# A token-mixing kernel: the second token matrix and three of eight pairs of the first in fp32 matmuls, without splits into fp16 parts

## The chip, the cores and the metric

The kernel runs on one core of a Trainium2 chip. The metric is the device time of one execution in microseconds; the median of three runs is compared. Engines are named as the profile does: PE is TensorE (PEld its weight loads), DVE is VectorE, ACT is ScalarE, SP is SyncE, which here only issues DMAs.

## What is computed

The inputs are a sequence `u` of 2048 tokens by 512 channels, the parameters of a state-space layer, and four weight matrices. The output is `x + s * g`:

```python
x = A_u
xn = _layernorm(x, axis=-1)
s = _A_ref(xn, ...)          # per channel: y = causal convolution of xn with K, plus xn * Dskip
g = _silu(_B_ref(xn, B_w1, B_w2, B_w3, B_w4))
return x + s * g

# _B_ref(x, w1, w2, w3, w4):
h = _gelu(_layernorm(x, axis=-1) @ w1)
# g0..g3: the four quarters of h's channels, shifted by +1, -1, +2, -2 tokens
hs = jnp.concatenate([g0, g1, g2, g3], axis=-1) @ w2
x1 = x + hs
h2 = _gelu(_layernorm(x1, axis=-1) @ w3) @ w4
return x1 + h2
```

`w1` and `w2` (512 x 512 each) are called the first and the second token matrix here. `K[d, l]` is the real part of a sum over 128 states of `C * exp(dt * A * l) * dt * B`, and the convolution in the reference goes by an FFT over 4096 points.

## The kernel before, in words

All 2048 tokens stay in SBUF as `X`, 128 partitions by 16 slots `s` by 512 channels; token = 16 * partition row + slot in each half, so a shift by one or two tokens is a step to another slot, and only the six combinations that run over the end (`WRAPS`, `wrapped`, line 1095) need rows moved, into `hw`.

The token mixing (`token_mixing`, line 1200) goes over eight pairs of slots. `ln_first` normalises (statistics on DVE; `E.affine` on ACT or DVE). `x_pair(j)` brings the normalised pair into `xT`, channels on the partitions: for `j < HF` in fp32, by four PE transposes a slot and a copy out of PSUM; for the others it is first split into two fp16 parts (`x2h`: a scaled rounding, then a `scalar_tensor_tensor` on DVE for the rest) and transposed by a DMA. `h_pair(j)` multiplies by w1: for `j < HF` 16 fp32 matmuls of 256 columns, else 48 fp16 matmuls (three products of parts, `PASSES`) with `w1h`, the split weights from `first_weights`. Then comes Gelu into `h32`, and `hT`, the result split into two fp16 parts again (one `affine`, one `scalar_tensor_tensor`). `HF` is 1, so only the first pair is in fp32. `u_stage1` multiplies two slots by a 64-point transform in fp32 and stores the result to DRAM (`ue`, then `scr_Ud`, 32 stores).

`second_weights` (line 976) finds w2's scale and splits w2 into `w2h`. `hs_pair` (line 1108) then takes the shifted slots of `hT` as the weights of PE and streams `w2h`: for each of 16 slots 4 channel blocks times 3 products of 512 columns, 192 fp16 matmuls in all, into two banks of `pa` or `pb`; DVE adds them into `X` with the scale `a2`. `hs` in this document is this step.

Beside it run two other streams. `tables` makes the convolution kernel in 16 chunks of 32 channels: on DVE and ACT the waves (`wv`), on PE 64 small fp32 matmuls (`pc<-wv`) and, after a copy into `kev`, eight more (`kev,kk`). `weight_squares` and `prep` load w3 and w4 (`wst`), find their scale and split them (`w3h`, `w4h`). After the token mixing, `mlp` runs eight times: six steps of matmuls on `w3h`, Gelu (`g`), a split (`ghl`) and matmuls on `w4h`. `products` multiplies spectra (`uin`, `kin`, `pr`, `z1e`), `inverse` and `finish` end with the gate, the residual and the store.

The order of all this is not the order of the code. Each call is recorded as an operation by `Plan.add`, and `Plan.order` (line 300) issues them in the order of the long list of numbers `ORDER` (line 110): a number is an operation, and a letter behind it chooses ACT (`a`) or DVE (`v`) where both can do it. Each engine works through its own instructions in that order. All instructions are issued from one line, 315, so the profile's rows are told apart by the names of the tiles.

Of the kernel before, what the change touches and what calls it, by code (L numbers as in the profile page):

```python
# [19 lines left out]
P = 128  # L20
# [31 lines left out]
HF = 1  # L52
# [58 lines left out]
5 0 8 7 3 88 89 6 79 80 81 82 90 91 92 93 83 2 94 95 22 21 105 84 85 9 106 86 103 96a 87a 97a 31 78 104 107 108 109  # L111
110 98 122 10 123 111 112 113 114v 115v 100v 119v 99a 124 116a 120 11 125 19 126 4 127 16 20 36 117 128 129 130 131
132 133 135 101 102a 134 138a 140a 136 38 18 37 137 17 152 158a 154a 39 42 40 14 153a 72 73a 139 15 70 71a 41 44 43 45
147 148 142 596 46 143 141 597 24 23 170 172 176 157a 174 177 173 604 205 47 149 175 171 155 48 49 178 50 144 160 51
150a 145a 159 179 52 180 211a 210a 53 181 182 118 121 195 196 54 146 156 207a 206a 183 59 151 25 26 245 200 201 202 27
184 185a 186a 243 189a 28 55 208 239 60 241 164 197 190 198v 230 192a 242 213 188a 56 246 187a 193 212 236a 209 240
310 235a 232a 231a 274 191 308 244 214a 194 225 311 237 312 309 220 221 314 13 598 313 234 315 61 57 226 247 62 316
248 317 249 233 203a 63 250 318 319 58 251 76 215 65 217a 606 238 280a 279a 64 252 320 204 253 218 66 68 29 255v 321
254v 275a 67 276a 299 216 199 222 219 264 261a 599 322 227 324a 281 256v 282 305a 304a 69 74 631 325a 396 265 269 277
270 258v 223v 259 228v 262 257v 278 300a 224 266 167 161 75a 162 229 271 301v 77a 601 30 397 602 260 600 283v 263 286a  # L120
272v 343 267a 294 284 273 302 287 323a 303 344a 268 603 306 32 295 307 296 289 297v 345a 632 290 349a 609 285 605 348a
368 327a 328 288 330v 346 338 298 291 607 331 350 351 608 329 373a 292v 615 347 370a 610 369a 339 352v 332 374v 326v
355a 618 375 293 333 334 335 387 376 392a 398 399 168 611 633 336a 400 337 163 401 402 340 356 372 403 341v 404 612
353 613 405 371 354 614 389a 424 393a 342 388a 358 406 165 407 409 166 408 169 425 363 364 410 411v 413v 412 634 414
616 359 483 482 637 426 427 487 499 428 429 635 430 395 636 617 484 498 619 620 640 621 33 432 431 434 433 435 622 485
638 659 448 449 34 488 450 360 361a 357 639 436 377 378 500 35 438 437 451 642 452 453 503 653 454 365 366a 382 654
379 641 662 383 439 440 442 441 384 491 495 380a 444 385a 490 386 513 391 623a 624 367 381 486 446 445 655 455 492 443
447 460 517 456 461 421 422 362 457 462 501 423 418 419 458 463 496 656 657 658 512 476 459 493 420 464 465 12 514 518
625 626a 643 627a 628a 644 489 645a 525 394 466 494 506 504 515 467 505 660 629a 468 675 516 469 676 502 507a 519 677
477a 473 497 390 520 479 478 509 521 415 416 524 538 417 1 529 678 646 526 630 679 680 508 522 661 681 470 535 480a  # L130
523 588a 589a 539 592a 682 546 593a 481 540 647 648a 649a 650a 543 561 663 664 684 665 536a 474 651a 705 697 590 532
666 683 698 667a 668 533a 560 510a 547 591 594 707 708 595 669 710 565 798 799 819a 686 709 652 699 537 568 562 805
670a 471 701 800 671a 672a 673a 806 807 700 702 511 685 687 703 472 688 801a 534 704 812 813 551 548 711 554 802 803
712 555a 556 814 732 557 820a 821 822 827 828 569a 570 834 835 577 804 558a 559 713 574 808a 809 810 714 811 706 719
716 733 715 717 689a 690 815a 816 734 823a 575a 578a 576 475 829 830a 718 824a 691 674 692a 571 825 817 693a 572a 694a
695a 720 721 741 841 842 818 735 836 837a 831 738 737 736 722 723 826 848 849 754 855 724a 755 856 579 696 756 739 757
573 758 838 832 833 839 843a 725 740 759 850 726 727a 844 840 845 742 743 760 744 745 851a 852 857 858a 934 859 869a
# [49 lines left out]
class Plan:  # L187
# [229 lines left out]
def kernel(  # L417
# [897 lines left out]
```

## Time and profile before

| | |
|---|---|
| runs | 535.85, 534.35, 536.67 us; median 535.85 |
| the profiled execution | 536.33 us, its span 534.5 us |
| mean granted clock of PE | 0.965 |
| ACT_TABLE_LOAD on ACT | 54 |
| DMA issues w2 and w1 (`w`) | 4 of 512 KB |

A row of the profile that groups instructions reads: line, engine, operation, tile written <- tiles read, shape, count, then after the bar the group's busy time in us and the mean duration of one record in ns, then the idle time ahead of them and who ended it. Matmul records overlap, so the group's busy time over its count is the price of one, not the mean record. An fp32 matmul leaves two records. A row of the timeline begins with its start and its length in us. A row of the stages gives a stretch, its length and each engine's busy time in it.

### The profile page before, as it was taken

Reading aid. Unit: us, or ns where it says so; the run is one execution under the profiler, and the core shown is the slowest. Engines: PE = TensorE matmul, PEld = TensorE weight load, DVE = VectorE, ACT = ScalarE, POOL = GpSimd, SP = SyncE. Lnnn points to the kernel's source line nnn. Section 1 sums busy time; section 2 is a strip of 40 time slices with the busy share of each in tenths; the row PEclk is TensorE's granted clock in tenths of the full one; section 3 lists DMA queues with packets and bytes.
Section 4 is the critical chain, followed back from the end, with each engine's and each line's share of the span. In section 5 each row is a group of like instructions: output and inputs, shape, how many; then the busy total and the mean of one; then the engine's idle time right before and its main releaser. Section 6 shows DMA issues by size and latency. Waiting matters only on the chain.

```text
span 534.5 us, 14802 instructions
## 1 busy us (share of the span) xinstructions
PE 486.1 (91%) x6292; PEld 311.9 (58%) x6292; DVE 476.8 (89%) x773; ACT 417.1 (78%) x699; POOL 0.7 (0%) x6
## 2 busy tenths in 40 slices
PE   8876986879989989999999999999999999899984
PEld 8552754554536745756657665666656665566542
DVE  4999699999999999999999999999998588667466
ACT  4899789988799999999999999998874634352520
POOL 0000000000000000000000000000000000000000
PEclk9795989999889989999999999999999999999998
DMA  8797785875457454440354660877679999996997
GB/s 234 177 229 198 203 207 140 229 200 163 119 118 155 101 108 104 61 60 14 49 101 80 139 171 21 187 143 172 144 156 190 268 319 236 264 309 204 341 307 195
DMA packets 160658, 91.13 MB, mean 170 GB/s; under 512 B 102544, under 2 KB 151952, under 8 KB 160208
## 3 DMA queue, kind: packets, MB, share of 16 engines
q1 hardware_dynamic: 156064, 85.73, 64.4%
q10 hardware_dynamic: 4528, 4.46, 3.2%
q8 instruction: 49, 0.80, 0.7%
q14 instruction: 17, 0.14, 0.1%
HBM read 52.95 MB, written 29.36 MB: 154 GB/s over the span
## 4 chain that ended last, share of the span: by engine, by line
PE 42%; DVE 27%; ACT 18%; DMA 8%; issue 5%; SPq 0%; ACTq 0%; DVEq 0%
PE pb L315 14%; PE pa L315 14%; DVE wv L315 11%; PE pc L315 8%; ACT wv L315 7%; PE pd L315 5%; DVE X L315 4%; DMA x1T<-x1h 2%; ACT L315 2%; DVE ghl L315 2%; ACT ue L315 1%; DVE pr L315 1%; DMA zin<-scr_Zda 1%; DMA scr_Ud<-ue 1%; ACT wst L315 1%
## 5 line engine op out<-in xcount | busy, mean ns | idle before, releaser
L315 PE MATMUL pb<-x1T,w3h 128*128 128x256 f16 (+1 forms) x1056 | 125.3, 274 | 3.4 <-issue 1.3
L315 PE MATMUL pa<-w4h,ghl 128*128 128x512 f16 (+1 forms) x528 | 123.3, 382 | 0.0
L315 PEld LDWEIGHTS <-w3h 128*128 128x128 f16 (+1 forms) x1056 | 101.9, 100 | 30.0 <-issue 15.4
L315 PEld LDWEIGHTS <-ghl 128*128 128x128 f16 (+1 forms) x528 | 49.6, 98 | 61.1 <-issue 9.3
L315 ACT ACT_TABLE_LOAD x54 | 69.3, 1283 | 11.5 <-PE pb L315 4.3
L315 ACT ACTIVATE wv<-wv 128x2080 f32<-128x2080 int32 x32 | 63.0, 1968 | 1.7 <-DVE wv L315 1.6
L315 ACT ACTIVATE g<-pb,wsc 128x512 f32<-128x512 f32 (+1 forms) x48 | 31.0, 655 | 14.9 <-PE pb L315 9.3
L315 PE MATMUL pb<-xT,w1h 128*128 128x256 f16 x336 | 39.6, 279 | 0.0
L315 PEld LDWEIGHTS <-w1h 128*128 128x128 f16 x336 | 32.9, 100 | 9.4 <-issue 2.9
L315 DVE TENSOR_TENSOR wv<-wv,eg 128x2048 f32<-128x2048 f32 x16 | 36.5, 2281 | 0.5 <-ACT wv L315 0.5
L315 PE MATMUL pc<-wv 128*32 128x64 f32 x2048 | 34.3, 225 | 2.9 <-ACT k1e L315 1.4
L315 PEld LDWEIGHTS pc<-wv 128*32 128x32 f32 x2048 | 31.4, 113 | 8.7 <-issue 2.5
L315 DVE TENSOR_TENSOR wv<-mag,wv 128x2048 f32<-128x2048 f32 x16 | 36.5, 2280 | 0.0
L315 DVE SCALAR_TENSOR_TENSOR ghl<-g,wsc,ghl 128x512 f16<-128x512 f32 (+1 forms) x48 | 33.6, 700 | 0.6 <-ACT ghl L315 0.3
L315 ACT ACTIVATE wv<-wv,halfpi 128x2080 f32<-128x2080 f32 x16 | 32.8, 2050 | 0.1
L315 ACT ACTIVATE mag<-par 128x128 f32<-128x128 f32 x132 | 32.5, 461 | 0.0
L315 PEld LDWEIGHTS <-hT 128*128 128x128 f16 x174 | 17.2, 99 | 24.9 <-issue 6.1
L315 DVE TENSOR_TENSOR pr<-pd,kh 128x512 f32<-128x512 f32 x32 | 20.6, 683 | 7.5 <-PE pd L315 5.9
L315 ACT ACTIVATE ghl<-g,wsc 128x512 f16<-128x512 f32 (+1 forms) x37 | 25.4, 691 | 1.5 <-PE pa L315 1.4
L315 DVE BATCH_NORM_STATS2 stats<-X 128x6 f32<-128x512 f32 x32 | 21.3, 679 | 5.2 <-DMA X<-in_A_u_dram 5.2
L315 DVE TENSOR_TENSOR wv<-par,ev 128x1056 int32<-128x1056 f32 x16 | 20.0, 1248 | 5.7 <-PE pc L315 5.7
L315 PE MATMUL pb<-w2h,hT 128*128 128x512 f16 x87 | 21.1, 395 | 2.6 <-DVE X L315 2.6
(158 smaller groups left out, 845.7 us busy)
## 6 DMA issues: line engine op xcount, KB each, us to landing
wst<-in_B_w_dram SPq DMA_DIRECT2D x20, 512.0 KB, 4.2
scr_Ud<-ue SPq DMA_DIRECT2D x32, 256.0 KB, 3.1
uin<-scr_Ud SPq DMA_DIRECT2D x16, 512.0 KB, 5.2
scr_Kfa<-k1e SPq DMA_DIRECT2D x8, 512.0 KB, 5.6
cst<-c_gp SPq DMA_DIRECT2D x16, 256.0 KB, 4.3
kin<-scr_Kfa SPq DMA_DIRECT2D x8, 512.0 KB, 5.2
scr_Kfb<-k1e SPq DMA_DIRECT2D x8, 512.0 KB, 6.7
scr_Zda<-z1e SPq DMA_DIRECT2D x8, 512.0 KB, 4.5
```

Source lines behind the costliest of these rows:

```text
L315: ins = [getattr(self.engines[op.eng], name)(*args, **kw).ins for name, args, kw in op.calls]
```

## The change

`HF` goes from 1 to 3: pairs 1 and 2 of the first token matrix take the way of pair 0, fp32 with PE transposes. `h_pair` writes `hT` in fp32 straight from Gelu, without `h32` and without parts, for all eight pairs. The second token matrix is used in fp32 as it was loaded: `second_weights`, `w2h` and the scales `s2`, `i2`, `a2`, `sh` are gone, `hs_pair` issues 64 fp32 matmuls, and DVE adds without a scale. w2 is loaded to the place that `w2h` had. `hw` holds one fp32 part instead of two fp16 ones. `ORDER` is a new list.

```diff
-HF = 1
+HF = 3
...
 ORDER = """
-5 0 8 7 3 88 89 6 79 80 81 82 90 91 92 93 83 2 94 95 22 21 105 84 85 9 106 86 103 96a 87a 97a 31 78 104 107 108 109
+8 31 0 7 88 3 4 78 89 90 91 22 21 103 105 106 104 92 107 108 2 109 6 93 94 95 5 79 110 111 96a 100a 80 81 82 83 14 112
...
-    hw = at(gtile.o, [P, 6, 2, P], F16, "hw")
+    hw = at(gtile.o, [P, 6, P], F32, "hw")
...
-        load_w(w2, w2s, Slots(sblocks + 10 * K4, sblocks + 11 * K4), Q)
+        load_w(w2, w2s, w2place, Q)
...
-        V.tensor_scalar(sh, s1, 2.0 ** -10, None, op0=ALU.mult)
...
-    def second_weights():
-        due("wq2")
-        for k in range(2):
-            w = wides[2 + k]
-            A.activation(at(phB + 4 * K4, [P, 2, D], F32, "sq"), w, AF.Square, accum_out=ssq[:, 14 + k : 15 + k])
-        pow2_scale(ssq[:, 14:16], s2, i2, 2.0 ** 14)
-        V.tensor_scalar(a2, i2, i1, 2.0 ** 10, op0=ALU.mult, op1=ALU.mult)
-        for k in range(2):
-            w = w2place([P, 2, 2, D], F16, "w2h")
-            E.affine(w[:, :, 0], wides[2 + k], s2)
-            V.scalar_tensor_tensor(w[:, :, 1], wides[2 + k], s2, w[:, :, 0], op0=ALU.mult, op1=ALU.subtract)
-            w2h.append(w)
...
-        h = stile([P, 4, 2, 2, P], F16, "hT")
+        h = stile([P, 4, 2, P], F32, "hT")
...
-            h32 = wtile([P, 2, 2 * P], F32, "h32")
-            A.activation(h32, ph, AF.Gelu_apprx_tanh, scale=1.0 if j < HF else a1)
-            E.affine(hv[0], h32, sh)
-            V.scalar_tensor_tensor(hv[1], h32, sh, hv[0], op0=ALU.mult, op1=ALU.subtract)
+            hv = h[:, 2 * m2 : 2 * m2 + 2].rearrange("p m a t -> p m (a t)")
+            A.activation(hv, ph, AF.Gelu_apprx_tanh, scale=1.0 if j < HF else a1)
...
-                    for n, (lh, lw) in enumerate(PASSES):
-                        T.matmul(
-                            acc[i], w[:, lh], w2h[m // 2][:, m % 2, lw],
-                            start=m == 0 and n == 0, stop=m == 3 and n == 2,
-                        )
+                    T.matmul(acc[i], w, w2s[m], start=m == 0, stop=m == 3)
...
-            V.scalar_tensor_tensor(X[:, s], acc[i], a2, X[:, s], op0=ALU.mult, op1=ALU.add)
+            V.tensor_add(X[:, s], X[:, s], acc[i])
...
-        second_weights()
```

Where the new list moves instructions, the prediction shows the rows on SP and on PE. The SP rows shown there are those around the load of w_103, one half of w2, among the stores `scr_Ud` of stage 1; the PE rows are those around the small matmuls `pc<-wv` of the fourth chunk of tables, which stood behind the first matmuls on `w3h` and now stand ahead of them.

Before, on PE, where the second token matrix begins, each matmul has a row of its weights ahead of it:

```order
L315 MATMUL pb_94<-xT,w1h 128x256
L315 LDWEIGHTS hT
L315 MATMUL pa_92<-w2h,hT 128x512
L315 LDWEIGHTS hT
L315 MATMUL pa_92<-w2h,hT 128x512
```

And now, where the fp32 matmuls stand as one row each and the two halves of w2 follow each other:

```order
L312 MATMUL pb_93<-xT,w1h 128x256
L312 MATMUL pa_92<-w_103,hT 128x512 x2
L312 MATMUL pa_92<-w_104,hT 128x512 x2
L312 MATMUL pa_91<-w_103,hT 128x512 x2
L312 MATMUL pa_91<-w_104,hT 128x512 x2
L312 MATMUL pc_96<-wv 32x64 x64
```

Three rows of four blocks of fp16 parts have become one row for two blocks; the first chunk's table matmuls follow after the first pair of slots.

More of the change, by code (lines that the diff above doesn't have):

```diff
@@ L116 @@
[L116 to L125, printed above, removed]
@@ new lines @@
+113v 84 85 86 17 115v 44 16 42 114a 87a 15 41 43 97a 20 101 98 36 45 46 18 37 118a 72 102a 47 99v 116 48 50 9 51 121
+10 122 49 52 23 143 117a 123 53 124 125 54 119 24 164 170 166 171 140 168 25 73a 141 167 165 126 169 551 127 55 172
+128 59 173 120a 60 56 11 146 174 175 142 129 19 38 151a 176 27 61 177 57 130 178 39 179v 152a 180v 26 182v 183v 33
+148a 144 40 181v 184 186a 131 62 229 28 187 145 147a 192 161 204v 185a 231 154 158 290 188a 132 134 288 70 205 553 150
+149 230 292 156 227 153 195 197a 196v 200a 286 375 232 225 287 291 289 71a 293 228 226 294 543 233 295 162 234 544 296
@@ new lines @@
+133 235 201a 207a 189 208 373 297 298 199 136v 545 34 299 236 237 190 216 198 63 191 137 217a 193 210 374 202 300 138v
+218a 211 304v 203 221v 65 194 64 546 238 371 13 222a 66 68 206 256 135 220 239 219 376 212 139 554 213 67 242v 223
+240v 224 257a 258a 262a 261a 209 69 74 555 243v 30 75a 214 215 241v 259 260 277 244v 302v 250 251 278a 58 76 279a 253
+252 247v 263 157 264 283a 254 268v 282a 379 245 246 317 248 249 372 163 271 548 549 159 160 265a 547 280 269 550 77a
+380 272 556 557 301v 255 558 559 281 285 552 381 266 318a 319a 565 284 578 322a 323v 562 308v 274 275 270 329v 267 309
@@ new lines @@
+273 276 338 560 320 321 340a 561 579 314 325 324 377 339v 342 311 341 312 344a 303v 343a 353 580 330 581 29 346 563
+584 564 378 315 355a 354a 305a 306 382 566 395 567 430 434 587 583 582 345 585 429 568 383 384 358a 385 386 387 155
+431 326a 586 388 569 600 396 397 601 570a 359a 446 389 390 606 445 316 391 392 602 35 393 394 407 589 310 398 408 409
+447 410 313 450 307 603 605 435 332 604 399 400 327 411 412 333 335 451 413 32 571 588 12 572 573a 336 401 334 432 609
+402 590 591 592a 607 331 448 337 328 622 360 623 361 453 608 347 403 624 348 611 350 351 349 362 438 404 414 610 631
@@ new lines @@
+711 712 846 809 731 700 824 825 826 732 810 811 853 847 800 801 812a 713 714 715a 880 854 807 808 813 814 831 815 832
+855 716 821a 856 857 849 923 717 718a 838 719a 499 848 819 850 851 822 827a 833 852 823 733 734 858 859 735 736 737a
+828 829 830 496 1215 839 860 861 834a 488 720a 721a 477 862 901 902 1222 1223 863 1216 1217 491 840a 474 835 903 738
+739 722 740a 741a 836 837 864 867 1224 865 1229 742a 743a 744 1218a 841 866 1236a 842 1225a 882 904 1230 1231 843 1244
+868 869 870 1219 871 906 844 1220 1221 907 872a 944 945 905 873 874 910 875a 876a 1251 946 1226 877a 878a 883 881
@@ new lines @@
+1237a 1232a 1227 885a 908 1238 884a 947 948 886 1233 1228 949 1239 887 891 925 1252 888 1245 909 889 890 892 1240a
+1241a 893 1246 1234 1235 894 1242 895 898a 912 1258 1247a 879 911 950 953 896a 913 899a 1259 500 1253 1243 897a 914
+1265 1254a 1255 915a 900 924 916 917 918a 497 492 489 1266 919a 920a 1248 1249 475 987 478 988 921a 926 968 922 1267
+1279 1250 527 927a 951 528 989 928a 529 952 530 929 934 1256 1257 930 1260a 936 990 992 1280 935 931 991 1268a 1272
+937 1273 932 1281 954 933 1274 938 1009 940a 1261 1286a 955 993 1262 956 957 1269 994 1030 941a 1287a 939a 942a 943
@@ new lines @@
+1263 1031 1275a 1301 1302 1288 958a 1276 959 960 1264 1038 995 961a 962a 963a 964a 996 1043 1270 1271 966 997 969
+1290a 1277 1282a 1283 971a 970a 1040 1041 998 1289 967 972 973 1011 977 974 978 975 976 979 1042 1278 1294 1284 980
+965 981 983a 985a 1032 984a 1035 982v 1033 1034 986 1036 1037 1295 1296 999 1052 1044 1000 1001a 1002 1045 1010 1285
+1297a 1298 1291a 1292 1086 1087 1303 1304a 1305 1003 1004a 1005a 1308 1309 1293 1006a 1007a 1008 1039 1088 1299 1046
+1012 1014a 1013a 1300 1306 1015 1049 1322 1310a 1311 1016 1020 1017 1315 1048 1021 1022 1023 1065 1018 1019 1047 1050
@@ new lines @@
+1051 1316 1317 1053 1307 1054 1323 1318a 1312 1024 1108 1067 1089 1324 1025a 1026a 1336a 1329 1330 1319 1092 1091 1055
+1056 1313 1057a 1028a 1027a 1029 1066 1095 1058 1314 1344 1345 1090 1059 1320 1129 1321 1130 1060a 1061a 1062a 1093
+1063a 1337a 1338 1339 1068 1325a 1326 1331 1327 1328 1332a 1094 1333 1131 1069a 1070a 1071 1064 1076 1072 1078 1340a
+1346 1341a 1077 1347a 1348 1342 1343 1351 1352 1358 1073 1074 1132 1334 1075 1079 1134 1080 1151 1097 1096 1084a 1083a
+1081a 1082a 1085 1335 1098 1099 1133 1138 1100a 1349 1350 1135 1359 1136 1110 1353 1101 1102 1103a 1104a 1137 1172
@@ new lines @@
+1365 1105a 1106a 1111 1354a 1113a 1355 1112a 1173 1174 1366 1109 1114 1356 1115 1153 1119 1367 1357 1175 1177 1360v
+1116 1379 1361 1362 1120 1117 1118 1121 1122 1123 1124a 1127a 1125a 1368a 1140 1139 1126v 1380 1141 1176 1369 1363
+1142 1181 1372 1143a 1144 1364 1145 1107 1146a 1147a 1373 1178 1179 1180 1148a 1149a 1128 1152 1738 1737 1739 1154
+1156a 1155a 1196 1370 1194 1374 1157 1162 1158 1163 1381 1159 1160 1371 1382a 1161 1386a 1394 1401 1150 1387a 1164
+1165 1166 1168a 1183 1167a 1402 1169a 1170a 1171 1182 1388 1184 1185 1186v 1187 1389 1395 1396 1188 1375v 1376 1377
@@ new lines @@
+1189a 1383 1507 1190a 1191a 1192a 1197 1195 1390a 1391a 1378 1397v 1198a 1398 1199a 1200 1205 1201 1207 1202 1193 1403
+1408 1206 1203 1208 1204 1384 1385 1399 1392 1508 1209 1509 1211a 1393 1409 1400 1213a 1210a 1404v 1528 513 514 1212a
+1405 1510 1512a 510 511 1513 1511v 1514 1679 1677 1530 1518 1736 1515 1516 1517 1422 1519 1551 1423 1520 1521 1529
+1415 1522 1549 1424 1523a 1416 1410v 1524a 1214 1531 1532a 1525v 1526v 1527 1534 1411 1535 1533a 1550 1539 1406 1536
+531 1537 1538 1540 1541 1542 532 1407 1412 1413 1414 1417 1425v 1418a 1543 533 1591 1572 1544v 534 1436v 1546a 1419
@@ new lines @@
+1692 1449 1687 1625 1685 1621 1622 1626 1627 1460v 1454v 1455 1628a 1631v 1629v 1461 1630v 1466 1467 1636 1637v 1638a
+1639 1740 1678 1640 1632 1479 1681 1480 1644 1641 1611 1450 1645 1642 1741 1643 1646 1647 1648 1650v 1649a 1657 1658v
+1651a 1652a 1660 1684 1661 1659a 1456 1457 1665 1663 1662 1666 1462 1653 1667 1668 1742 1743 1664 1669 1670v 1673a
+1473 1672v 1671a 1674 1693 1695 1714 1689 1705 1694 1481 1493 1494 1474 1486 1487 1464 1468a 1475v 1676 1748 1744 1691
+1690 1702 1696 1698 1706 1488 1700 1463 1469 1470 1471 1718 1725 1476 1477 1478 1755 1784 1500 1482a 1704 1483 1699
@@ L184 @@
+1495 1484 1489a 1490 1501 1759 1707 1708 1719 1703 1709 1713 1712 1715 1485 1496a 1491 1492 1502v 1497 1498 1682 1720
[3 rows of a table added]
 """
@@ L924, in pow2_scale @@
         V.tensor_scalar(dst_inv, dst_inv, 1.0 / float(target), None, op0=ALU.mult)
-    s3, i3, s4, i4, sg, ig, a3, a4, s1, i1, a1, s2, i2, a2, sh = [
-        wsc[:, k : k + 1] for k in range(15)
-    ]
+    s3, i3, s4, i4, sg, ig, a3, a4, s1, i1, a1 = [wsc[:, k : k + 1] for k in range(11)]
     w3t, w4t = [], []
@@ L958, in weight_scales @@
         V.tensor_mul(a4, ig, i4)
-    w1h, w2h = [], []
+    w1h = []
     def first_weights():
@@ L1067, in h_pair @@
                             )
-            hv = [h[:, 2 * m2 : 2 * m2 + 2, k].rearrange("p m a t -> p m (a t)") for k in range(2)]
-            h32 = wtile([P, 2, 2 * P], F32, "h32")
-            A.activation(h32, ph, AF.Gelu_apprx_tanh, scale=1.0 if j < HF else a1)
-            E.affine(hv[0], h32, sh)
-            V.scalar_tensor_tensor(hv[1], h32, sh, hv[0], op0=ALU.mult, op1=ALU.subtract)
+            hv = h[:, 2 * m2 : 2 * m2 + 2].rearrange("p m a t -> p m (a t)")
+            A.activation(hv, ph, AF.Gelu_apprx_tanh, scale=1.0 if j < HF else a1)
     def u_stage1(s):
```

90 lines of the change are left out of this document (23 added, 67 removed), and 6 rows, old and new, of the table ORDER.

## The prediction

> **What bounds the kernel now.** I read the profile page first, then the busy time by stage, the groups of instructions by form, the timeline of TensorE, and what stands ahead of each wait. The page gives the profiled execution: its span, the busy time of each engine, the granted clock.
>
> ```profile
> span 534.5 us, 14802 instructions
> PE 486.1 (91%) x6292; PEld 311.9 (58%) x6292; DVE 476.8 (89%) x773; ACT 417.1 (78%) x699; POOL 0.7 (0%) x6
> PEclk9795989999889989999999999999999999999998
> ```
>
> No engine is clearly the bound over the whole span: TensorE (PE) 91%, VectorE (DVE) 89%. So I cut the span into four stages at events that both orders have: A up to the first matmul of the second token matrix (98.8), B up to the first matmul on w3h (167.8), C up to the end of the last chunk's tables (411.2), D the rest. The columns are the stage, its length, then busy time (and instructions) of PE, PE's weight loads, DVE, ACT and POOL, the clock, the DMA share and GB/s.
>
> ```profile
> 0.00:98.80 98.80, 79.36 (x494) 56.84 (x495) 83.66 (x204) 82.16 (x152) 0.70 (x6) 0.88 0.77 196
> 98.80:167.80 69.00, 61.41 (x678) 33.59 (x677) 66.99 (x107) 61.17 (x99) 0.00 (x0) 0.95 0.64 163
> 167.80:411.20 243.40, 235.80 (x3706) 156.31 (x3702) 241.05 (x294) 226.39 (x375) 0.00 (x0) 0.99 0.54 112
> 411.20:534.50 123.30, 109.55 (x1426) 65.15 (x1418) 85.08 (x171) 47.35 (x76) 0.00 (x0) 0.98 0.93 269
> ```
>
> In A, PE is idle for 19.4 us; DVE and ACT do more. In B, DVE is busy for 67.0 of 69.0 us, PE idle for 7.6. In C both are full, DVE with 2.4 us idle, PE with 7.6. In D, DVE and ACT have 38 and 76 us to spare, and PE is what is left. The timeline of PE shows what ends A, and where B ends:
>
> ```profile
> 40.67 2.08 PE L315 MATMUL pa<-X,ks 64*128 64x512 f32 x4 [3.88 <-ACT X L315]
> 58.27 1.13 PE L315 MATMUL pa<-X,ks 64*128 64x512 f32 x4
> 59.23 1.02 PE L315 MATMUL pd<-X,ks 64*128 64x512 f32 x4
> 98.84 10.52 PE L315 MATMUL pa<-w2h,hT 128*128 128x512 f16 x48 [1.55 <-ACT ue L315]
> 167.81 5.42 PE L315 MATMUL pb<-x1T,w3h 128*128 128x256 f16 x48
> ```
>
> A ends when ACT has copied a bank out (ue), so A's length is ACT's, and DVE's that feeds it. So the change takes work off DVE and ACT in A, where they set the pace, and puts work on PE in B and later, where PE has 7.6 us of room in 69.
>
> **The change part by part.** The rows by form carry the prices; the number behind the bar is the busy time of the group, so it is divided by the count. An fp32 matmul shows as two records (x32 for the 16 of the first pair).
>
> ```profile
> L315 PE MATMUL pb<-xT,w1h 128*128 128x256 f16 x336 | 39.6, 279 | 0.0
> L315 PE MATMUL pb<-xT,w 128*128 128x256 f32 x32 | 7.1, 379 | 0.0
> L315 PEld LDWEIGHTS pb<-xT,w 128*128 128x128 f32 x32 | 6.0, 190 | 0.8
> L315 PE MATMUL pd<-ident,x 128*128 128x128 f32 x8 | 1.7, 354 | 0.0
> L315 PE MATMUL pb<-w2h,hT 128*128 128x512 f16 x87 | 21.1, 395 | 2.6 <-DVE X L315 2.6
> L315 PE MATMUL pa<-w2h,hT 128*128 128x512 f16 x87 | 19.6, 379 | 1.6 <-ACT ue L315 1.6
> L315 PE MATMUL pb<-w2h,hw 128*128 128x512 f16 x9 | 3.0, 452 | 0.0
> L315 PE MATMUL pa<-w2h,hw 128*128 128x512 f16 x9 | 2.4, 379 | 0.0
> L315 PE MATMUL pb<-x1T,w3h 128*128 128x256 f16 x960 | 113.2, 273 | 3.4 <-issue 1.3 <-DMA x1T<-x1h 1.3 <-DVE w3h L315 0.7
> L315 PE MATMUL pa<-w4h,ghl 128*128 128x512 f16 x480 | 112.0, 383 | 0.0
> L315 PE MATMUL pc<-wv 128*32 128x64 f32 x2048 | 34.3, 225 | 2.9 <-ACT k1e L315 1.4
> ```
>
> *Second token matrix on PE.* Out go 192 fp16 matmuls, 21.1 + 19.6 + 3.0 + 2.4 = 46.1 us. In come 64 fp32 ones of 512 columns, which the trace does not show; the nearest row is the first pair's, 7.1 / 16 = 0.442 us for 256 columns, so 0.884 for 512 and 56.6 in all: +10.5. The other bound is the four half-height fp32 matmuls of 512 columns in 58.27 to 60.25, 1.98 us: if two of them together stand for one full one, 0.99 each, 63.4, +17.3. I take +10.5, the row of the same height and weights.
>
> *Two more pairs of the first matrix in fp32.* 96 matmuls of 39.6 / 336 = 0.118 us (11.3) become 32 of 0.442 (14.1): +2.8; and 16 transposes by PE at 1.7 / 8 = 0.21: +3.4, in place of four DMA transposes. PE in all: 10.5 + 2.8 + 3.4 = +16.7 us.
>
> *The splits.* These rows are what leaves DVE and ACT, with two rows of a chunk's tables for its price:
>
> ```profile
> L315 DVE SCALAR_TENSOR_TENSOR hT<-h,wsc,hT 128x512 f16<-128x512 f32 x16 | 11.8, 741 | 0.0
> L315 DVE SCALAR_TENSOR_TENSOR x2h<-X,rs,x2h 128x512 f16<-128x512 f32 x14 | 10.3, 737 | 0.6 <-ACT x2h L315 0.6
> L315 DVE TENSOR_SCALAR hT<-h,wsc 128x512 f16<-128x512 f32 x7 | 3.4, 479 | 1.2 <-ACT h L315 1.2
> L315 DVE SCALAR_TENSOR_TENSOR w2h<-w,wsc,w2h 128x1024 f16<-128x1024 f32 x2 | 2.5, 1280 | 0.0
> L315 DVE TENSOR_SCALAR w2h<-w,wsc 128x1024 f16<-128x1024 f32 x2 | 1.4, 746 | 0.0
> L315 ACT ACTIVATE hT<-h,wsc 128x512 f16<-128x512 f32 x9 | 6.3, 722 | 0.1
> L315 ACT ACTIVATE X<-X,bs,rs 128x512 f32<-128x512 f32 x9 | 7.2, 810 | 0.4 <-ACT rs L315 0.3
> L315 DVE TENSOR_TENSOR wv<-wv,eg 128x2048 f32<-128x2048 f32 x16 | 36.5, 2281 | 0.5 <-ACT wv L315 0.5
> L315 DVE TENSOR_TENSOR wv<-up,wv 128x1024 f32<-128x1024 f32 x16 | 19.4, 1214 | 0.0
> ```
>
> DVE loses 11.8 + 3.4 + 2.5 + 1.4 and four of the x2h (2.9): 22 us; ACT loses 6.3 and two squares. The new order hands DVE some of ACT's work back (13 normalisations of X instead of 7 stand on DVE, both w1h scalings). My count of rows times these durations leaves DVE 14 us and ACT 17 us lighter over the span. How it falls on the stages is in the order. On SyncE (SP), which issues the loads in order, w_103 is a half of w2 and scr_Ud are the stores of stage 1 of u. Before:
>
> ```order
> L315 DMA scr_Ud<-ue 256x1x256 x3
> L315 DMA w_103<-in_B_w_dram 128x2x512
> L315 DMA_TRANSPOSE xT<-x2h 128x8x128 x2
> L315 DMA scr_Ud<-ue 256x1x256 x4
> L315 DMA w_104<-in_B_w_dram 128x2x512
> ```
>
> Now:
>
> ```order
> L312 DMA scr_Ud<-ue 256x1x256 x4
> L312 DMA wst<-in_B_w_dram 128x4x256
> L312 DMA scr_Ud<-ue 256x1x256 x2
> L312 DMA w_103<-in_B_w_dram 128x2x512
> L312 DMA scr_Ud<-ue 256x1x256 x2
> ```
>
> The load of w_103 has moved from behind 12 of the 32 stores to behind 26. The 25th to 28th stores were issued from 85.56 in the timeline below, and the page's median from issue to landing is 5.5 us; at the old pace w_103 lands at about 92.
>
> ```profile
> 85.56 2.52 SPq L315 DMA_DIRECT2D scr_Ud<-ue  x4
> w<-in_B_w_dram SPq DMA_DIRECT2D x4, 512.0 KB, 5.5
> ```
>
> On PE, the matmuls pc<-wv of the fourth chunk of tables. Before, they stand among the first matmuls on w3h, in C:
>
> ```order
> L315 MATMUL pb_93<-x1T,w3h 128x256
> L315 MATMUL pc_95<-wv 32x64 x64
> L315 LDWEIGHTS w3h
> L315 MATMUL pb_94<-x1T,w3h 128x256
> L315 LDWEIGHTS w3h
> ```
>
> Now they stand among the second token matrix's, in B:
>
> ```order
> L312 MATMUL pb_93<-w_104,hT 128x512 x2
> L312 MATMUL pc_95<-wv 32x64 x64
> L312 MATMUL pa_91<-w_103,hT 128x512 x2
> L312 MATMUL pa_91<-w_104,hT 128x512 x2
> L312 MATMUL pb_94<-w_103,hT 128x512 x2
> L312 MATMUL pb_94<-w_104,hw 128x512
> ```
>
> So a whole chunk has moved from C to B: on PE 34.3 / 16 = 2.1 and its second step 1.2, 3.3 us; on DVE two steps of 2.28 and seven of 1.21 to 1.25, 13 us. Counted in the order, 48 matmuls on w1h have also moved from A to B (5.7), and 12 on w3h and 24 on w4h from C to D (12 x 0.118 + 24 x 0.233 = 7.0).
>
> *The sum by stage.* A: PE -144 x 0.118 + 14.1 + 3.4 = +0.5, on 79.4; DVE 8 and ACT 11 us lighter. Bounds 88 (all of ACT's 11) and 98.8 (w_103 and start-up hold it); I take 93, just past the landing. B: PE 61.4 + 10.5 + 5.7 + 3.3 = 80.9; DVE 67.0 + 11.5 = 78.5. Bounds 81 (PE never idle) and 95 (its 7.6 us of idle stay, and the dearer fp32 price); I take 84. What is queued behind a late fp32 group is DVE's add into X, and behind that the table work, so DVE cannot run ahead. C: PE 235.8 - 10.3 = 225.5, DVE 241.0 - 21.4 = 219.6; PE is now the fuller. Bounds 225.5 and 233.1 (with the 7.6 idle); I take 231. D: 123.3 + 7.0 = 130.3, bounds 128 and 131. Sum 93 + 84 + 231 + 130.3 = 538.3, or +3.8 us on the span of 534.5. The profiled execution took 536.33, 1.83 more than its span, and lies 0.48 over the median of 535.85; the median would be 535.85 + 3.8 = 539.7, so 540.
>
> **The rivals.** *Faster: DVE leads and PE follows.* For it: DVE is idle for 2.4 us of C, and PE records stretch (0.118 us a matmul on w3h over the span, 5.42 / 48 = 0.113 in the piece at 167.81), so PE may have more room than it shows. Then C goes with DVE's work, 243.4 x 219.6 / 241.0 = 222, A gives all of ACT's 11, B is 81, D 130: 521, 13 below, time 522. Against it: PE's 16.7 us are more than the 15.2 that it idles in B and C together, and D only grows. It decides from the point where B plus C come under 309. The Trainium skill (Perfetto Trace Analysis, Identifying the Most-Contended Engine) speaks for it: matmul busy time is a poor measure, and the share of weight loads should be used. By that measure PE, at 58%, has room, DVE is the bound, and the time would be this rival's. The rows of B and C, where PE idles 3 to 11%, bear it out only in part.
>
> *No change.* A at 93, B near its floor (82), C at 229: 534, +-2.7. For it: the three stages each need only a microsecond or two.
>
> *Much slower: PE waits in B.* hs on w_103, which lands late, and PE idle as before: A 97, B 95, C 233, D 131 = 556, time 557. The row of fp32 weight loads (190 ns each, two to a matmul, 0.8 us of idle for 32) says that the loads hide. The Trainium skill (TensorE: Matmul & The Clock Gate, Weight-path perf modes) says that fp32 weights get no fast load; were all 128 loads of the second matrix in the open, that estimate would add 128 x 0.19 = 24 us to B; the pair in the trace shows them hidden.
>
> **How the numbers follow.** My forecast, slower by some 4 us, has 0.45, with a likeliest range of 534 to 546; no change 0.19; DVE leads 0.26; PE waits 0.10. About 0.5%, 2.7 us, is what a measurement of this kernel can tell from no change. A quarter of the forecast's own range lies within that (0.11), three quarters beyond it (0.34); of the case of no change a tenth spills over to slower (0.02). So slower by over 0.5%: 0.34 + 0.10 + 0.02 = 0.46; within: 0.11 + 0.17 = 0.28; faster: 0.26. The range takes in the bounds of A, B and C short of all of them at once, and leaves out the far ends of the two outer rivals: 527 to 550.
>
> **What would show it.** Right: the first matmul of the second matrix near 93 and the first on w3h near 177; fp32 matmuls of 512 columns at 0.88 us; B with PE over 95% busy; PE busy sum near 500; the last chunk done near 408. Wrong: w3h starting before 170 (B not bound by PE), C shorter than 225, or DVE still with under 1% idle in C, which would be the first rival.

## The result, and the profile after

The changed kernel takes 515.5 us (median of four, 514.98 to 516.05), the one before 535.1 beside it (533.58 to 536.67): a ratio of 0.9634, 95% interval 0.9601 to 0.9666. That is 3.7% faster, and below the predicted range of 527 to 550. The profiled execution took 514.98 us, its span is 513.1. The page has these lines where that of before had 534.5, 486.1, 476.8 and 417.1:

```profile
span 513.1 us, 14564 instructions
PE 491.4 (96%) x6209; PEld 315.6 (62%) x6209; DVE 461.7 (90%) x744; ACT 403.4 (79%) x675; POOL 0.7 (0%) x6
PEclk9899999999999999999999999999999999999998
```

PE does more, DVE and ACT less, as forecast in sign; PE's rise is 5.2 us where 16.7 was forecast. But PE's idle time has fallen from 48.4 us to 21.7, and the slice at half clock (the 5 in the clock's row of before) is gone. The same four stages, A to D, with the columns of the prediction's table:

```profile
0.00:81.70 81.70, 72.73 (x428) 54.50 (x428) 73.44 (x176) 72.65 (x139) 0.70 (x6) 0.98 0.97 242
81.70:161.90 80.20, 80.04 (x807) 43.79 (x808) 79.67 (x123) 73.93 (x119) 0.00 (x0) 1.00 0.60 143
161.90:387.60 225.70, 222.94 (x3524) 149.09 (x3522) 220.42 (x270) 203.73 (x337) 0.00 (x0) 1.00 0.54 114
387.60:513.10 125.50, 115.64 (x1458) 68.18 (x1454) 88.20 (x178) 53.10 (x82) 0.00 (x0) 0.98 0.90 265
```

Against before, A is 17.1 us shorter, B 11.2 longer, C 17.7 shorter, D 2.2 longer: -21.4. In B, PE is busy for 80.04 of 80.20 us and DVE for 79.67; in C, PE has 2.8 us left, where it had 7.6. Where B begins and ends, on PE's timeline:

```profile
81.68 7.13 PE L312 MATMUL pa<-w,hT 128*128 128x512 f32 x16 [0.83 <-ACT ue L312]
90.79 7.03 PE L312 MATMUL pa<-w,hT 128*128 128x512 f32 x16
161.89 8.02 PE L312 MATMUL pb<-x1T,w3h 128*128 128x256 f16 x72
```

Eight fp32 matmuls (16 records) take 7.03 us, 0.88 each. Over all 64 the groups by form give 26.4 + 26.3 + 3.2 + 3.1 = 59.0 us, 0.92 each:

```profile
L312 PE MATMUL pb<-w,hT 128*128 128x512 f32 x58 | 26.4, 596 | 0.0
L312 PE MATMUL pa<-w,hT 128*128 128x512 f32 x58 | 26.3, 597 | 0.8 <-ACT ue L312 0.8
L312 PE MATMUL pb<-w,hw 128*128 128x512 f32 x6 | 3.2, 610 | 0.0
L312 PE MATMUL pa<-w,hw 128*128 128x512 f32 x6 | 3.1, 592 | 0.0
```

What became of A is seen in slices of 20 us. First three of before, then three of after:

```profile
20.00:40.00 20.00, 16.80 (x100) 12.67 (x96) 19.08 (x36) 17.97 (x37) 0.00 (x0) 0.93 0.80 190
40.00:60.00 20.00, 15.33 (x76) 8.29 (x76) 16.95 (x51) 19.91 (x39) 0.00 (x0) 0.68 0.86 233
60.00:80.00 20.00, 18.43 (x123) 12.34 (x122) 16.64 (x29) 14.32 (x26) 0.00 (x0) 0.91 0.67 174
```

```profile
20.00:40.00 20.00, 17.52 (x85) 12.67 (x84) 19.93 (x53) 19.85 (x47) 0.00 (x0) 0.98 0.81 192
40.00:60.00 20.00, 19.30 (x97) 12.78 (x96) 19.96 (x62) 19.91 (x46) 0.00 (x0) 1.00 1.03 264
60.00:81.70 21.70, 20.44 (x154) 14.14 (x152) 20.39 (x24) 21.63 (x31) 0.00 (x0) 1.00 1.08 272
```

Before, DVE leaves 3 us idle in each of the slices from 40 to 80 us, and ACT 5.7 in the last of them; after, both are nearly full from 20 us on (DVE has 1.3 us left in the last slice). For DVE that is 83.66 busy and 15.1 idle in 98.8 us before, 73.44 and 8.3 in 81.7 after: 10 us of work and 7 of waiting have gone. Its waits in A before:

```profile
DVE stats L315 <- DMA X<-in_A_u_dram: 5.2, 2, 4.2
DVE wv L315 <- PE pc L315: 4.5, 1, 4.5
DVE hT L315 <- ACT h L315: 1.2, 1, 1.2
```

After, only the first loads are still waited for, and one wave:

```profile
DVE stats L312 <- DMA X<-in_A_u_dram: 5.5, 2, 3.1
DVE wv L312 <- ACT wv L312: 1.1, 1, 1.1
```

One more thing has moved in A that the prediction did not price. The split weights `w1h` were needed by pair 1; now three pairs go by without them. The first matmul on `w1h` before, and after:

```profile
31.38 5.42 PE L315 MATMUL pb<-xT,w1h 128*128 128x256 f16 x48
```

```profile
57.75 2.79 PE L312 MATMUL pb<-xT,w1h 128*128 128x256 f16 x24
```

The first matmul on `w1h` starts 26 us later.

### The profile page after: what moved, and what is told of

Same layout as the page of the kernel before. It is cut to its first block, busy times and chain, and to the rows that moved or that the text cites. A ratio compares the mean times of both kernels' runs of the same rounds, so it can differ in the third digit from the quotient of the medians.

```text
span 513.1 us, 14564 instructions
## 1 busy us (share of the span) xinstructions
PE 491.4 (96%) x6209; PEld 315.6 (62%) x6209; DVE 461.7 (90%) x744; ACT 403.4 (79%) x675; POOL 0.7 (0%) x6
## 4 chain that ended last, share of the span: by engine, by line
PE 54%; DVE 35%; ACT 5%; issue 3%; DMA 1%; SPq 0%; DVEq 0%; ACTq 0%
PE pb L312 23%; PE pa L312 16%; DVE wv L312 13%; PE pc L312 10%; PE pd L312 5%; DVE X L312 5%; DVE stats L312 2%; DVE pr L312 2%; DVE ghl L312 2%; DVE eg L312 1%; ACT L312 1%; DVE tm L312 1%; ACT wv L312 1%; DVE kh L312 1%; DMA X<-in_A_u_dram 1%
## 5 line engine op out<-in xcount | busy, mean ns | idle before, releaser
L312 PEld LDWEIGHTS pc<-wv 128*32 128x32 f32 x2048 | 29.8, 109 | 6.6 <-issue 2.4
L312 PE MATMUL pc<-wv 128*32 128x64 f32 x2048 | 32.4, 220 | 0.7 <-DVE wv L312 0.6
L312 PE MATMUL pb<-xT,w1h 128*128 128x256 f16 x240 | 27.7, 273 | 0.0
L312 PE MATMUL pa<-w,hT 128*128 128x512 f32 x58 | 26.3, 597 | 0.8 <-ACT ue L312 0.8
L312 PEld LDWEIGHTS <-w1h 128*128 128x128 f16 x240 | 22.8, 98 | 6.0 <-issue 2.6
L312 PE MATMUL pb<-w,hT 128*128 128x512 f32 x58 | 26.4, 596 | 0.0
L312 ACT COPY z1e<-pc 128x256 f32<-128x256 f32 x24 | 8.7, 381 | 21.6 <-PE pd L312 21.6
```

The source lines that it names most:

```text
L312: ins = [getattr(self.engines[op.eng], name)(*args, **kw).ins for name, args, kw in op.calls]
```

## The experiments

The theories. *Work*: the splits filled DVE and ACT; without them these run ahead and PE closes up, whatever the order. *Order*: the new list brings the gain. *Clock*: PE without gaps keeps its clock, which shortens A. The runs, with their stages as above (the first matmul of the second matrix, the first on `w3h`, the last of the chunks); the ratio is to the kernel before on the same chip:

| run | us | ratio (95%) | A | B | C | D |
|---|---|---|---|---|---|---|
| before | 535.1 | 1 | 98.8 | 69.0 | 243.4 | 123.3 |
| after | 515.5 | 0.963 (0.960-0.967) | 81.7 | 80.2 | 225.7 | 125.5 |
| arith_in_old_order | 556.0 | 1.036 (1.030-1.042) | 109.9 | 78.2 | 243.5 | 122.8 |
| old_order_new_engines | 564.6 | 1.057 (1.050-1.063) | 107.1 | 76.6 | 250.5 | 128.3 |
| old_arith_in_new_order | 600.3 | 1.120 (1.114-1.126) | 143.1 | 103.0 | 229.8 | 125.1 |
| quarter_out | 518.1 | 0.965 (0.960-0.971) | 82.5 | 77.8 | 230.2 | 125.2 |
| adds_out | 514.5 | 0.961 (0.956-0.967) | 81.2 | 79.8 | 225.4 | 125.2 |
| both_out | 514.2 | 0.962 (0.956-0.968) | 81.5 | 77.8 | 226.9 | 125.6 |
| vector_load | 524.3 | 0.981 (0.978-0.984) | 86.2 | 84.7 | 225.3 | 125.6 |
| splits_back | 551.0 | 1.026 (1.021-1.032) | 103.3 | 93.1 | 226.0 | 125.1 |
| splits_later | 543.5 | 1.017 (1.014-1.020) | 95.7 | 95.5 | 225.5 | 125.3 |
| kept_warm | 536.2 | 1.001 (0.998-1.004) | 97.4 | 67.2 | 244.6 | 122.2 |
| second_alone | 529.8 | 0.992 (0.990-0.995) | 96.4 | 80.2 | 225.9 | 125.3 |
| second_alone_w1_early | 525.1 | 0.982 (0.978-0.986) | 91.7 | 80.2 | 227.7 | 125.5 |
| w1_early | 521.6 | 0.975 (0.970-0.979) | 89.1 | 80.2 | 226.1 | 125.1 |
| four_pairs | 522.0 | 0.977 (0.972-0.982) | 92.0 | 81.4 | 224.6 | 125.5 |
| chunk_back | 667.2 | 1.248 (1.239-1.257) | 82.1 | 88.0 | 368.9 | 125.7 |

### The two halves apart

**arith_in_old_order**, the changed code with the list of before (numbers for operations it lacks are dropped):

```diff
 ORDER = """
-8 31 0 7 88 3 4 78 89 90 91 22 21 103 105 106 104 92 107 108 2 109 6 93 94 95 5 79 110 111 96a 100a 80 81 82 83 14 112
+5 0 8 7 3 88 89 6 79 80 81 82 90 91 92 93 83 2 94 95 22 21 105 84 85 9 106 86 103 96a 87a 97a 31 78 104 107 108 109
```

> The changed kernel's arithmetic (second matrix and three pairs in fp32, no splits), in the order and with the ACT/DVE choices of the kernel before; 20 operations that had no place in that order or would wait in a circle stand where their inputs are ready. Work theory (the splits paced the first stage; with them gone DVE and ACT run ahead and PE closes up, whatever the order): 514 to 521, the first stage 80 to 86 us. Order theory (the gain is the new list's): 531 to 538. Clock theory (a denser PE keeps its clock): as the work theory, but with the granted clock of the first stage over 0.95 where the time falls and near 0.88 where it does not.

555.98 us: no theory expected that. Its B, C and D:

```profile
109.85:188.00 78.15, 75.52 (x615) 38.62 (x616) 65.39 (x107) 59.56 (x99) 0.00 (x0) 0.96 0.54 132
188.00:431.50 243.50, 235.34 (x3707) 155.79 (x3704) 240.11 (x291) 225.76 (x371) 0.00 (x0) 0.99 0.53 112
431.50:554.30 122.80, 109.33 (x1422) 65.28 (x1418) 84.89 (x170) 47.39 (x76) 0.00 (x0) 0.98 0.92 270
```

C and D are those of before. B is 9 us longer, PE nearly full (75.5 of 78.2) and DVE with 12.8 us of room, about the 13 us of the chunk of tables that the new order puts there. The work theory falls with its "whatever the order": in this list the new arithmetic costs 19 us (3.55% of 535). As 20 operations stand here in a list that was not made for them, the 19 us are no price of the arithmetic alone.

**old_order_new_engines**, that kernel with ACT or DVE chosen as after:

```diff
-114v 100v 118v 99a
+114a 100a 118a 99v
```

> The first run of this study again (the changed kernel's arithmetic in the order of before, 555.98 us), but with the choice of ACT or DVE for each operation that the changed kernel makes (69 choices differ). If the 40 us between that run and the changed kernel are the uneven load of ACT (80.0 busy) and DVE (66.2) in its first stage of 110: 530 to 540. If they are the places in the order: 550 to 560.

564.6, over both ranges: with ACT (71.0) and DVE (72.9) even in A, A is still 107.1. The places are at fault, not the uneven load.

**old_arith_in_new_order**, the code of before with the new list:

```diff
 ORDER = """
-5 0 8 7 3 88 89 6 79 80 81 82 90 91 92 93 83 2 94 95 22 21 105 84 85 9 106 86 103 96a 87a 97a 31 78 104 107 108 109
+8 31 0 7 88 3 4 78 89 90 91 22 21 103 105 106 104 92 107 108 2 109 6 93 94 95 5 79 110 111 112 96a 100a 80 81 82 83 14
```

> The arithmetic of the kernel before (all splits, fp16 products) in the changed kernel's order; the operations that only it has stand right behind what they need, 52 have had to move. Work theory: 530 to 545, first stage 93 to 100 us. Order theory: 513 to 522, first stage 80 to 86.

600.3, far outside both ranges, but with a C and D near those of after:

```profile
246.10:475.90 229.80, 224.49 (x3523) 149.97 (x3524) 222.28 (x271) 205.24 (x339) 0.00 (x0) 0.99 0.55 114
475.90:601.00 125.10, 115.37 (x1456) 68.19 (x1454) 88.12 (x178) 53.09 (x82) 0.00 (x0) 0.99 0.91 264
```

With the new arithmetic the list makes all of C's difference (243.5 to 225.7), with the old one 13.6 us of it (243.4 to 229.8); D's 2 us go with the list too. In the rows by form, DVE's tables in C (`wv`, `eg`, `up`, `pab`, `EB`, `rem`, `par`) fall from 170 us before to 153 after, and rise by 15 in B and 4 in A: the list has moved them forward. A and B of these crossed kernels say little on either half, since the operations without a place of their own wait there.

### What sets the second stage

**quarter_out** leaves out the fourth channel block of the second product, so it does not compute the whole result:

```diff
-                for m in range(4):
+                for m in range(3):
...
-                    T.matmul(acc[i], w, w2s[m], start=m == 0, stop=m == 3)
+                    T.matmul(acc[i], w, w2s[m], start=m == 0, stop=m == 2)
```

> The changed kernel with the last of the four channel blocks of the second token matrix left out: 16 of the 64 fp32 matmuls, some 14.4 us of PE at 0.9 each; everything else and the order stay. If PE alone is now the bound of the second stage: 501 to 503, that stage 66 us. If DVE (79.7 of its 80.2 us busy) holds it as well: 510 to 515, that stage 77 to 80. If neither, and what stands there is the order's waits: in between.

**adds_out** has DVE add 8 of 512 columns and leaves out the rest:

```diff
-            V.tensor_add(X[:, s], X[:, s], acc[i])
+            V.tensor_add(X[:, s, :8], X[:, s, :8], acc[i][:, :8])
```

> The changed kernel in which DVE adds only 8 of 512 columns of the second token product into X (the rest of that sum is left out): some 10 us of DVE less, nearly all in the second stage, PE and the order as they are. If PE's busy time is a floor there (80.0 of 80.2): the second stage stays 79 to 80.5, the time 513 to 516. If DVE sets its length and PE only looks full: second stage 70 to 74, 506 to 509.

**both_out** is both edits.

> Both at once: the fourth channel block of the second product left out (14.4 us of PE) and DVE adding only 8 of 512 columns (10 us of DVE). If PE and DVE are two floors of the same height in the second stage, neither edit alone shortens it and both together do: second stage 66 to 71, and 503 to 509 in all unless the transfers behind it (x1T) hold the third. If something else (ACT at 74, the tables' own chain) sets it: 76 and over, 513 to 518.

B of quarter_out, of adds_out and of both_out:

```profile
82.54:160.29 77.75, 67.37 (x774) 37.53 (x775) 77.60 (x122) 72.39 (x118) 0.00 (x0) 1.00 0.58 143
```

```profile
81.22:160.97 79.75, 79.75 (x806) 43.81 (x807) 73.54 (x123) 73.95 (x119) 0.00 (x0) 1.00 0.59 144
```

```profile
81.45:159.20 77.75, 70.14 (x774) 39.23 (x775) 71.71 (x122) 71.75 (x117) 0.00 (x0) 0.96 0.57 143
```

With 12.7 us less on PE, DVE is busy for 77.60 of 77.75, and PE ends B with a wait of 2.3 us for `x1T`. The time, 518.1, lies above the ranges named for PE and for DVE, because C is 4.5 us longer than after; 2.9 us of this is a wait of PE for the load `uin`. With 6.1 us less on DVE, PE is full. With both lighter, no engine is full and B still is 77.8: what ends it is a transfer.

```profile
159.21 3.15 PE L312 MATMUL pb<-x1T,w3h 128*128 128x256 f16 x14 [2.58 <-DMA x1T<-x1h]
```

The chain that leads to this matmul (start, length, engine or DMA, tile) shows what stands ahead of the transfer:

```profile
147.55 1.06 ACT w4h L312
148.64 1.28 DVE w4h L312
149.92 0.60 DVE x1h L312
150.52 2.31 DVE wv L312 x2
152.83 1.21 DVE w3h L312
154.05 0.37 SPq L312
154.47 4.60 DMA x1T<-x1h
```

From 118.94 to 148.61 this chain is all ACT. The last `x1h` is ready at 150.5, but its transpose stands on SP behind two loads of `wst`, and the second of them goes out only behind DVE's split of w3, at 154.05. The transfer itself takes 4.6 us.

So B has three floors within 2.5 us: PE's work at 80.0, DVE's list at 77.6, and at 77.8 a path through ACT's list, DVE's weight splits, SP's queue and a transfer. Taking 12.7 us off PE alone gains nothing in the whole time, and taking 6.1 off DVE alone gains nothing clear of noise either (514.5 against 515.5).

### What the splits of h are worth

**vector_load** puts DVE's half of the work back, without a partner to wait for:

```diff
+            x_n = X[:, 2 * j + m2]
+            V.scalar_tensor_tensor(spl.rearrange("p a t -> p (a t)"), x_n, sh, x_n, op0=ALU.mult, op1=ALU.subtract)
```

> The changed kernel with only the second half of the h splits put back as bare work: 16 scalar_tensor_tensor on DVE of some 0.74 us, 11.8 in all, behind each Gelu, reading a slot of X that has long been ready and writing a tile that nobody reads, so that DVE waits for nobody because of them. If DVE is full in the first two stages (no wait for another engine behind the start in the first, 79.7 of 80.2 us in the second): 11 to 13 more, 526 to 529. If DVE has room there: under 6 more, 515 to 521. If even bare work breaks the order, as the splits themselves did (35 more): 535 and over.

**splits_back** and **splits_later** put the real work back, right behind each Gelu and some operations later:

```diff
+            E.affine(spl, hv, sh)
+            V.scalar_tensor_tensor(spl, hv, sh, spl, op0=ALU.mult, op1=ALU.subtract)
```

> The changed kernel with the work of the splits of h put back beside it, into a tile that nobody reads: 16 scalings (7 to 9 on each of ACT and DVE) and 16 scalar_tensor_tensor on DVE, some 15 us of DVE and 6 of ACT; PE's work and the order of everything else stay. Work theory (DVE and ACT paced the first stage): 524 to 531, nearly all of it in the first two stages. Order theory and clock theory (DVE's load matters little): 515 to 518.

> The changed kernel with the whole work of the h splits, as in the run before last with it (16 scalings on ACT and DVE, 16 scalar_tensor_tensor on DVE), but each scaling some 8 operations and each scalar_tensor_tensor some 14 operations of the list behind its Gelu instead of at once. If the 35 us there were the work (DVE 15, ACT 6): again 545 to 552. If 15 were work and 20 the waits of one engine for the other right behind the Gelu: 528 to 536.

A and B of vector_load:

```profile
0.00:86.21 86.21, 71.78 (x428) 53.31 (x428) 79.22 (x187) 73.48 (x140) 0.70 (x6) 0.98 0.88 227
86.21:170.88 84.67, 80.36 (x806) 43.73 (x807) 84.42 (x130) 73.53 (x118) 0.00 (x0) 1.00 0.57 138
```

DVE's busy time is 5.8 us up in A and 4.8 in B, and both stages are 4.5 longer: work added to DVE goes into the time at over 0.8 to one. No run adds work to PE in the changed kernel, so the same may hold there. The 524.3 us lie between the ranges of the expectation, nearest to a full DVE. The whole splits cost 35 us at once (over both ranges) and 28 later (between the two), for 15 us of DVE and 6 of ACT, so more than work is paid. In splits_later DVE and ACT wait for each other:

```profile
DVE spl L314 <- ACT spl L314: 8.9, 3, 4.9
ACT spl L314 <- DVE spl L314: 9.7, 3, 6.3
```

That they use one tile in turn adds to it, so the size holds for this form alone.

### The clock

**kept_warm** is the kernel before with idle matmuls ahead of two quads of stage 1 (a quad is four fp32 matmuls on `X,ks` in a row, eight records):

```diff
+            if k == 0:
+                for j in (2, 3):
+                    due(f"wm{j}")
+                    with plan.together(cost=2.0):
+                        for _ in range(14):
+                            T.matmul(pt[:, :P], ident, ident, start=True, stop=True)
```

> The kernel before with 14 idle matmuls of 128 columns on PE in each of the two gaps of 4 us ahead of the third and fourth quads of stage 1 (40.7 and 48.5 us), into a bank that nobody reads then. If the clock is a cause of the first stage's length: those quads take 2.0 instead of 3.8 us, and the time falls by 2 to 4 us, to 531 to 533. If ACT and DVE pace that stage: the quads may be shorter, the time stays within 1 us of before.

The first halves of the two quads take 1.13 us, where the first took 2.08 before (the prediction's row at 40.67):

```profile
34.50 3.29 PE L315 MATMUL pc<-ident 128*128 128x128 f32 x28
39.09 1.13 PE L315 MATMUL pa<-X,ks 64*128 64x512 f32 x4 [1.30 <-ACT X L315]
41.01 3.39 PE L315 MATMUL pc<-ident 128*128 128x128 f32 x28
46.87 1.13 PE L315 MATMUL pa<-X,ks 64*128 64x512 f32 x4 [2.47 <-ACT ue L315]
```

The ratio is 1.0012, interval 0.9979 to 1.0044: no difference. PE waits for ACT all the same. The idle matmuls bring the clock of A from 0.88 to 0.93, and in both slices from 20 to 60 us to 1.00, without a gain; so the 0.98 of after reads as a consequence of PE's shorter waits, not as the cause of the shorter A.

### The three pairs and w1

**second_alone** is the changed kernel with one pair in fp32:

```diff
-HF = 3
+HF = 1
```

> The changed kernel with HF back at 1: the second matrix in fp32 and no splits of h, but pairs 1 and 2 of the first matrix split and in fp16 as before; the new order, in which 10 operations have moved. DVE gets four x2h of 0.74 (3 us) back and ACT or DVE four squarings, PE loses 6 us. If the second matrix and the splits of h carry the gain: 514 to 522. If the two pairs carry much of it: 525 to 535.

**w1_early** moves the scale and the split of `w1h` forward in the order, and the scaling from DVE to ACT:

```diff
 L312 COPY xT<-pd_97 128x4x128
+L312 ACTIVATE w1h<-w_101,wsc 128x2x512
+L312 ACTIVATE w1h<-w_102,wsc 128x2x512
...
+L312 SCALAR_TENSOR_TENSOR w1h<-w_101,wsc,w1h 128x2x512
 L312 SCALAR_TENSOR_TENSOR pn<-rawA,ld 128x512
```

> The changed kernel with one thing of its order undone: w1's scale and split (the two halves of w1h) stand early, as before, ahead of the transposes of the second pair's end, and on ACT for the scaling; the first matmul on w1h stays where it is (57.75 us). Theory of the late deadline (with three pairs in fp32 nobody needs w1h before 57 us, and its 5 us of DVE and ACT work is out of the way of the first slots of X): 3 to 8 us slower, 519 to 524, all of it in the first stage. If it does not matter when that work is done: 514.5 to 517.

**second_alone_w1_early** is both:

> The second matrix alone in fp32 (one pair of the first, as before) in the new order, but with w1's scale and split early, as the kernel before has them, so that pair 1 need not wait for them and no operation has to move. If the 14 us that the second matrix alone lacked were only w1h coming late: 514 to 521. If the two pairs in fp32 carry it for other reasons too (squarings and x2h on ACT and DVE, DMA transposes): 522 to 528.

**four_pairs** goes the other way (`HF = 4`):

> The changed kernel with a fourth pair of the first matrix in fp32: PE 3 us more (16 fp32 matmuls of 0.44 for 48 of 0.118, 8 transposes of 0.21), two x2h of 0.74 and two squarings less on DVE and ACT, two copies of xT more; five operations of the order have moved. If DVE and ACT set the first stage: 513 to 516. If PE (72.7 of 81.7 us busy there) or the order is disturbed: 517 to 522.

All four differ from after in A, and elsewhere by 2 us at most (the table). second_alone lies 14 us above after; with `w1h` early, where its pair 1 can use it, 4.7 of these come back (525.1). A of w1_early, and its longest wait on PE (1.2 us after):

```profile
0.00:89.07 89.07, 75.42 (x427) 56.52 (x428) 73.24 (x174) 75.25 (x141) 0.70 (x6) 0.92 0.87 222
```

```profile
PE pd L312 <- DVE x L312: 6.5, 1, 6.5
```

DVE does no more than after (73.2 us) and ACT 2.6 us more, yet A is 7.4 longer: the split of w1 stands ahead of the third pair's `x`, and PE waits 6.5 us for it. On ACT the scaling of w1 takes 2.19 us and waits 2.37 for its scale, and the statistics (`rs`) that `x` needs stand behind it. So doing this work at 29 to 35 us instead of 43 to 51 costs 6 us (521.6 against 515.5) in this list; another early place may cost less. The late place is open without a wait only because pairs 1 and 2 go without `w1h`. Between w1_early and second_alone_w1_early lie 3.5 us more, for the pairs themselves. Those have four `scalar_tensor_tensor` of 0.74 less on DVE, which at vector_load's 0.8 is 2.4 of them. A fourth pair loses 6.5 us in this list, which was not made for it; no version here that computes the whole result beats the changed kernel.

### One that failed

**chunk_back** moves the tables from the fourth chunk on to later places:

```diff
-L312 MATMUL pc_95<-wv 32x64 x64
 L312 MATMUL pa_91<-w_103,hT 128x512 x2
...
+L312 MATMUL pc_95<-wv 32x64 x32
 L312 MATMUL pb_94<-x1T,w3h 128x256
```

> The changed kernel with one other thing of its order undone: the tables from the fourth chunk on stand later, so that the matmuls of the fourth chunk again stand among the first on w3h, in the third stage, and the later chunks follow closer; 47 operations have moved besides. If the tables taken out of the third stage are what shortened it (DVE 241 us full there before, 220 now): second stage 70 to 78, third 233 to 243, together 4 to 12 us longer, 520 to 528. If the place of that chunk does not matter: 514 to 517.

667.2 us. With the tables 47 other operations moved. The last chunk now ends at 539 us, and C takes 368.9, of which PE is busy for 264.6 and DVE for 235.1: this is a spoilt order and says nothing on the chunk. That the chunk's move is what shortens C rests on the crossed kernels and the rows of tables above; its price alone was not measured.

## Why the prediction was wrong

The sign was wrong, by one step made four times: the prediction worked out the work, which came out nearly right, and then kept 35 us of PE's idle time from the old profile (538.3 less its PE sums of 79.9, 80.9, 225.5 and 116.6), where 21.7 are left.

- *Work.* DVE -14 was -15.0, ACT -17 was -13.7. PE's busy sums for B, C and D were 80.9, 225.5 and 116.6, and are 80.0, 222.9 and 115.6; only A's, 79.9, is well off (72.7, below). The price of a 512-column fp32 matmul, 0.88, is 0.88 in the dense piece and 0.92 over all. These held.
- *A: 93, with bounds 88 and 98.8, came out at 81.7.* This is the step that failed: "Bounds 88 (all of ACT's 11) and 98.8 (w_103 and start-up hold it); I take 93, just past the landing". It gave A all of ACT's relief at best, took the waits between the engines for fixed, and let the load of w_103 land at 92 "at the old pace". 7 of DVE's 15 us of idle time went too, and the pace was not the old one: the load stands where the order put it, but the stores ahead of it came 10 us earlier (85.56 before). Issued at 76.63, it landed 4.0 us later, at 80.6, and A ends 1 us behind it, on ACT's `ue`:

```profile
75.36 1.21 SPq L312 DMA_DIRECT2D scr_Ud<-ue  x2
76.63 0.61 SPq L312 DMA_DIRECT2D w<-in_B_w_dram  x1
```

The runs name parts of this and not the whole: with three pairs in fp32 the split of w1 can stand later, and an early place for it costs 6 us; DVE's work counts, at 0.8 to one where it is added.

PE's busy time in A, forecast at 79.9, was 72.7: the matmuls of stage 1 (`X,ks`) took 25.4 us before and take 17.3, at a granted clock of 0.88 and 0.98. In kept_warm a higher clock was worth nothing by itself.
- *B: 84, lower bound 81, came out at 80.2.* PE has no idle time. The charge of 10.5 us of PE work was sound as a floor; the 3.1 us of idle time added to it were not. Two causes of the longer B stand side by side: in the old order, without the chunk, PE's work makes B 9 us longer (PE 75.5 of 78.2, DVE 65.4); in the new one DVE's floor, with the chunk moved in, lies only 2.4 us below PE's, so that B would be nearly as long with less PE work (quarter_out, 77.8).
- *C: 231, came out at 225.7*, its lower bound. PE's idle time, 7.6 us, was kept at 5.5 and is 2.8. The shorter C is in the main the order's, and its size by PE's work, 225.5, was foreseen.
- *D: 130.3, bound 128, came out at 125.5*: PE idle 9.9 instead of 13.8.

So 11.3 + 3.8 + 5.3 + 4.8 = 25.2 us, 538.3 less 513.1. Of the rivals, "DVE leads and PE follows" (522, chance 0.26) was right in sign and near in size. Its condition, B and C together under 309, came true at 305.9. That its time is so near is partly luck: its A (88) and D (130) were too long and its C (222) too short. Its picture holds in part: work added to DVE counts and a cut in PE's alone gains nothing, but a cut in DVE's alone gains nothing clear of noise either, and in adds_out PE is the floor. The Trainium skill (Perfetto Trace Analysis, Identifying the Most-Contended Engine), which would go by weight loads, gives PE 55% in B (43.8 of 80.2); adds_out shows that PE was full there. For the kernel before, the rule puts DVE first, which the outcome bears out better than the forecast. Of the three signs named against the forecast, w3h before 170 came true (161.9), though its reading, B not bound by PE, did not; C stayed over 225 and DVE idles for 2.3% of it.

What stays open is how much of A belongs to the arithmetic and how much to the list: either without the other is slower than before by 19 to 64 us (by the ratios), so only steps near the changed kernel could be priced (an early w1 6 us, the pairs 3.5, DVE's half of the splits 9). These prices hold in the new list, and nothing shows that they add up.

## What to carry to other kernels

Idle time between engines that are all near full is not a stock that a change leaves alone: work out the floors of each engine by stage, and put the lower bound of a stage at the highest floor, not at the old length less the work removed. Ask of each conversion not only what it costs but which deadline it moves: here the first use of w1's split came 26 us later. A list of issues made for one arithmetic does not measure another: crossed with the other's list, either arithmetic lost about as much as the whole change gains (19 against 20 us), or more (64).

## What the runs showed that was not expected

Keeping PE busy with 14 idle matmuls (28 records, 3.3 us) in a gap of 4 us nearly halves the first half of the quad behind it (2.08 to 1.13 us) and does not change the time. And with fp32 weights of 128 columns for every 512-column matmul, PE is busy for 80.04 of 80.20 us while it loads weights for 43.8: the loads are hidden, so the fast load that the Trainium skill (TensorE: Matmul & The Clock Gate, Weight-path perf modes) denies to fp32 is not missed here.
